# Seven products in place of eight for the second MLP layer of four groups, with a new order of casts, squares and stores

## The chip, the cores and the metric

The kernel runs on one core of a Trainium2 chip. The metric is the device time of one execution in microseconds (us). The kernel before takes 329.64 us in the median. Profiles show the span from the first to the last instruction, some 1.7 us shorter than the time. Engines are named TensorE (PE in the profile, its weight loads PEld), VectorE (DVE), ScalarE (ACT), GpSimd (POOL) and SP, the queue that issues most transfers.

## The reference, cut to what matters

Eight batches of eight heads go through a Nystrom attention with 32 landmarks, and the result goes through an MLP block with layer norm:

```python
x = attn_out.transpose(0, 2, 1, 3).reshape(8, 576, 512)      # 4608 rows of 512
xn = (x - mu) / np.sqrt(var + 1e-06) * g_ln
ch = np.maximum(xn @ w_ch1, 0.0) @ w_ch2                     # 512 -> 2048 -> 512
out = x + ch
```

## The kernel before

The 4608 rows are 36 blocks of 128, in nine groups of four blocks (0 to 8). The attention works on batches in sets: batch 0, batch 1, then set 0 (batch 2), set 1 (batches 3 and 4), set 2 (5 and 6), set 3 (7). The MLP is a generator. Each `fill(n)` takes n of its matmuls and puts them between the steps of the attention, so that TensorE has work while the small attention matmuls wait for other engines. All engines run in the order in which the program was written down.

```python
    # an MLP group: first layer 64 matmuls of 512 columns, second layer 64
    for m in range(MCH):                                     # 16
        psh = psM.tile([P, 512], FP32, name="psh", tag="pm") # three shared banks
        for c in range(KCH):                                 # 4
            MM(psh[:], w1_16[:, c, ts(m, P)], xnT[:, c, :], ...)
        act(hT[:, m, :], psh[:], AF.Relu)
    ...
    for u in range(4):
        for m in range(MCH):
            MM(pso[:], hT[:, m, ts(u, P)], w2_16[:, m, ts(part, n)], ...)
        dve.scalar_tensor_tensor(out=ot[...], in0=pso[:], scalar=rstds[g][:, u:u + 1],
                                 in1=x[...], op0=ALU.mult, op1=ALU.add)
        store(j, ot, ts(part, n))                            # two issues on SP
```

Layer norm is split. Only the mean is taken off before the first layer (`center`, on GpSimd); 1/sqrt(var) is multiplied in after the second layer, because relu lets a positive factor through. For the variance ScalarE makes one `square` for each block. The main loop before (shortened):

```python
    fill(16)
    for c, after, plan in zip(sets, sets[1:] + [None], steps):
        while c.jobs:
            prepare(c, 1, 1)                 # one cast by GpSimd, one transpose or sum by VectorE
            fill(...)
        for (count, jobs), _ in zip(plan, attention2(c.bs, c)):
            fill(count)
            settle()                         # means and centers of finished blocks, by GpSimd
            a_square()                       # one square, by ScalarE
            if after:
                prepare(after, 1, jobs)      # one cast for the next set in every step
```

The softmax here doesn't subtract the row's maximum and nothing guards it: scores larger than these inputs give would overflow.

Of the kernel before, what the change touches and what calls it, by code (L numbers as in the profile page):

```python
# [20 lines left out]
def kernel(  # L21
# [20 lines left out]
    MCH = HID // P  # L42
    U = H // 4
    NJ = 9

    scale_qk = 1.0 / (D ** 0.5)
    sc_A = scale_qk / SEG
# [460 lines left out]
    class Coming:  # L508
# [89 lines left out]

        def spread(self, y):
            part = self.part.pop(y)  # L600
            psl = psM.tile([P, 2, 8, LM], FP32, name="psl", tag="pm")
            for half in range(2):
                MM(psl[:, half, :, :].rearrange("p k c -> p (k c)"),
                   spread16[:, half, :, :, :].rearrange("p e a w -> p (e a w)"),
                   part[:].rearrange("p n w r l x -> p (n w r l x)"))
            lm = asm.tile([P, 8, 2, LM], FP16, name="lm", tag="lm", bufs=3)
            scalar.copy(lm[:].rearrange("p k h c -> p h k c"), psl[:])
            for i, nm in enumerate(("q", "k")):
                for x in range(2):
                    self.lm[nm, 2 * y + x] = lm[:, ds(4 * i + 2 * x, 2), :, :].rearrange(  # L610
                        "p r h (l x) -> p r (h l) x", x=2)
# [118 lines left out]

        yield from rows_of(bs, ea, zcbd)

    ln_ready = {0}
    rowsum, variances, rstds, xn_of = {}, {}, {}, {}
    mlp_at, uncentered = [0], {}
    later, squares, negms = [], [], {}

    def settle():
        while later:
# [1 line left out]

    def block_done(j):
        g, u = divmod(j, 4)
        if g == 0:
            mean_of(j, dve)
            center(j, scalar if u % 2 == 0 else dve)
        elif g == 1:
            mean_of(j, dve)
            later.append(lambda: center(j, scalar))
        else:  # L750
            later.append(lambda: mean_of(j, pool))
            later.append(lambda: center(j, pool) if g <= mlp_at[0] + 1
                         else uncentered.setdefault(g, []).append(j))
        squares.append(lambda: square(j))
        if u == 3:
            if g == 1:
                later.append(lambda: ln_ready.add(1))
            squares.append(lambda: deviations(g))

    def mean_of(j, engine):  # L760
        negms[j] = mstat.tile([P, 1], FP32, name="negm", tag="negm", bufs=16)
# [3 lines left out]
    def center(j, engine):  # L765
        g, u = divmod(j, 4)
        xn_of[j] = xn = mxn.tile([P, DM], FP16, name="xn", tag="xn")
        if engine is scalar:
            act(xn[:], x_blk[j][:], AF.Identity, bias=negms[j][:], scale=1.0)
        elif engine is dve:  # L770
            dve.tensor_scalar(out=xn[:], in0=x_blk[j][:], scalar1=negms[j][:],
                              scalar2=None, op0=ALU.add)
        else:
            pool.tensor_scalar(out=xn[:], in0=x_blk[j][:], scalar1=1.0, scalar2=negms[j][:],
                               op0=ALU.mult, op1=ALU.add)
        if g < 2:
            return
        if u == 0:
            xnTs[g] = mxnT.tile([P, KCH, 512], FP16, name="xnT", tag="xnT")
        keep(nc.sync.dma_start_transpose(out=xnTs[g][:, :, ts(u, P)], in_=xn_of.pop(j)[:]))  # L780

    def square(j):
        g, u = divmod(j, 4)
        if u == 0:
            variances[g] = mstat.tile([P, 4], FP32, name="var", tag="var")
        junk = mxn.tile([P, DM], FP16, name="junk", tag="junk", bufs=1)
        act(junk[:], x_blk[j][:], AF.Square, bias=negms[j][:],
            accum_out=variances[g][:, u:u + 1])

    def deviations(g):  # L790
        lnv = mstat.tile([P, 4], FP32, name="lnv", tag="lnv")
        act(lnv[:], variances.pop(g)[:], AF.Ln, bias=eps_ln[:], scale=1.0 / DM)
        rstds[g] = mstat.tile([P, 4], FP32, name="rstd", tag="rstd")
        act(rstds[g][:], lnv[:], AF.Exp, scale=-0.5)
        ln_ready.add(g)

    def store(j, ot, cols):
        for i in range(2):
            b, c = divmod(2 * j + i, NJ)
            half = ot[ds(64 * i, 64), cols]  # L800
            to = out[b].rearrange("(t j) f -> j t f", j=NJ)[c][:, cols]
            nc.sync.dma_start(out=to, in_=half)

    xnTs = {}

# [15 lines left out]
            yield  # L821



    def mlp():
        for g in range(NGRP):
            mlp_at[0] = g
            hT = mhT.tile([P, MCH, 512], FP16, name="hT", tag="hT")
            if g == 0:
                for m0, u in ([(m, 0) for m in range(0, 12, 2)] + [(m, 2) for m in range(0, 12, 2)]  # L830
                              + [(m, u) for u in (0, 2) for m in (12, 14)]):
                    for t in {(0, 0): (0, 1), (8, 0): (2,), (10, 0): (3,)}.get((m0, u), ()):
                        transpose_block(0, t)
                        yield True
                    psh = psM.tile([P, 2, 256], FP32, name="psh", tag="pm")
                    for m in range(2):
                        for c in range(KCH):
                            MM(psh[:, m, :], w1_16[:, c, ts(m0 + m, P)],
                               xnTs[0][:, c, ds(P * u, 256)],
                               start=(c == 0), stop=(c == KCH - 1), skip=True)  # L840
                            if c == 1 or (c == 3 and m == 0):
                                yield True
                    act(hT[:, m0:m0 + 2, ds(P * u, 256)], psh[:], AF.Relu)
                    yield True
            else:
                while g == 1 and g not in xnTs:
                    if g in ln_ready:
                        for _ in transposes(g):
                            yield True
                    else:  # L850
                        yield False
                while g > 1 and g not in ln_ready:
                    yield False
                xnT = xnTs.pop(g)
                for j in uncentered.pop(g + 1, ()):
                    center(j, pool)
                for m in range(MCH):
                    psh = psM.tile([P, 512], FP32, name="psh", tag="pm")
                    for c in range(KCH):
                        MM(psh[:], w1_16[:, c, ts(m, P)], xnT[:, c, :],  # L860
                           start=(c == 0), stop=(c == KCH - 1))
                        if c < KCH - 1:
                            yield True
                    act(hT[:, m, :], psh[:], AF.Relu)
                    yield True
            tr = None
            for u in range(4):
                j = 4 * g + u
# [28 lines left out]
    def fill(n):  # L897
        for _ in range(n):
            if not next(stream, False):
                return  # L900
# [61 lines left out]
    def prepare(c, casts, jobs):  # L962
        for _ in range(casts):
            if c.casts and (c.parts[c.casts[0]][0] == "v" or len(c.n16) < 8):
                c.next_cast()
                while sum(len(x.stg) for x in sets) < (3):
                    left = [x for x in sets if x.loads]
                    if not left:
                        break
                    left[0].next_load()  # L970
        for _ in range(jobs):
            c.next_job()

    for _ in range(6):
# [1 line left out]

    fills = {"scores of k": 4, "gram": 5, "iteration": 4,
             "product": 5, "zc": 4, "rows": 6}
    def a_square():
        if squares:  # L980
            squares.pop(0)()

    n = 0
    for what in a1:
        fill(fills[what])
        settle()
        if what in ("iteration", "product"):
            a_square()
        if what in ("product", "zc", "rows"):
            n += 1  # L990
            prepare(sets[0], 1, 1 if n > 3 else 0)
    while len(sets[0].jobs) > 1:
        prepare(sets[0], 1, 1)
        fill(6)
    fill(16)

    steps = [[(10, 0), (12, 1)] + 6 * [(6, 1)] + [(8, 1)] + 5 * [(6, 0)]]
    steps += [[(6, 0), (8, 0), (12, 0), (12, 0), (6, 0), (6, 0), (5, 0), (5, 0), (5, 0), (5, 0), (8, 0)] + 3 * [(6, 0)] + 7 * [(7, 1)]]
    steps += [[(12, 0), (14, 1), (16, 1), (16, 1)] + 6 * [(9, 1)] + [(10, 1)] + 10 * [(8, 1)]]
    steps += [[(15, 0), (18, 0)] + 6 * [(12, 0)] + [(12, 0)] + 5 * [(12, 0)]]  # L1000
    for c, after, plan in zip(sets, sets[1:] + [None], steps):
        while c.jobs:
            prepare(c, 1, 1)
            fill(5 if c is sets[1] else 8)
        for (count, jobs), _ in zip(plan, attention2(c.bs, c)):
            fill(count)
            settle()
            a_square()
            if after:
                prepare(after, 1, jobs)  # L1010
    settle()
    while squares:
        a_square()
    for _ in stream:
        pass

# [29 lines left out]
```

## Time and profile before

| | before |
|---|---|
| time, median (lowest to highest) | 329.64 us (328.40 to 330.07) |
| span, mean granted clock | 327.9 us, 0.989 |
| TensorE busy | 312.7 us (95%), 3248 matmuls |
| VectorE, ScalarE, GpSimd busy | 147.7, 153.9, 126.6 us |

TensorE sets the time; the other engines are busy less than half of it. What counts are therefore the matmuls and the places where TensorE stands. The lines that show these are in the prediction.

### The profile page before, as it was taken

To read this page: it belongs to the slowest core of one execution; us is meant where nothing else is said; L and a number is where in the kernel's file an instruction comes from. 1 tells how busy PE (TensorE), PEld (TensorE's weight loads), DVE (VectorE), ACT (ScalarE), POOL (GpSimd) and SP (SyncE) were. 2 spreads that over 40 slices of the span, in tenths; PEclk is the share of its full clock that TensorE was granted. 3 is DMA by queue.
4 is the path that set the end of the run, shared out by engine and by line. 5 is a ranking of instruction groups with operands and counts; after the bars stand their busy time and mean duration, and the time that the engine had idled before them with its cause. 6 is when DMAs were issued, how large, how long until landed. Compare 5 with 4: busy or idle time off the path is not lost.

```text
span 327.9 us, 7900 instructions
## 1 busy us (share of the span) xinstructions
PE 312.7 (95%) x3248; PEld 157.5 (48%) x3248; DVE 147.7 (45%) x392; ACT 153.9 (47%) x301; POOL 126.6 (39%) x194
## 2 busy tenths in 40 slices
PE   8789999899977989999999999999999999999994
PEld 8568654444432534544454445444444444444443
DVE  2667249678782415799366346431232210010012
ACT  2466853587043671567505644583048316305600
POOL 4389879708994796448043011600010300000000
PEclk9999999999995999999999999999999999999999
DMA  7999999559959993933086003520341124032023
GB/s 265 395 386 385 386 389 281 161 109 388 200 133 292 381 246 88 209 113 65 10 213 162 0 18 80 98 35 2 71 98 25 33 67 93 2 79 50 2 56 72
DMA packets 38700, 50.32 MB, mean 153 GB/s; under 512 B 17540, under 2 KB 17800, under 8 KB 38664
## 3 DMA queue, kind: packets, MB, share of 16 engines
q1 hardware_dynamic: 38664, 49.82, 53.6%
q8 instruction: 25, 0.41, 0.6%
q14 instruction: 11, 0.09, 0.1%
HBM read 36.70 MB, written 9.44 MB: 141 GB/s over the span
## 4 chain that ended last, share of the span: by engine, by line
PE 77%; POOL 6%; DMA 5%; DVE 5%; issue 2%; ACT 2%; SPq 1%; POOLq 0%
PE psh L73 35%; PE pso L73 31%; DMA stg<-in_k_dram 2%; PE psy L73 2%; POOL asum L67 2%; PE psn L73 2%; PE pscv L73 2%; DMA xnT<-xn 2%; POOL nat L67 1%; POOL natv L67 1%; DMA stg<-in_q_dram 1%; DVE xblk L67 1%; PE psec L73 1%; DVE part L67 1%; SPq L780 1%
## 5 line engine op out<-in xcount | busy, mean ns | idle before, releaser
L73 PE MATMUL psh<-xnT,w 128*128 128x512 f16 (+1 forms) x640 | 136.3, 360 | 2.0 <-DMA xnT<-xn 2.0
L73 PE MATMUL pso<-w,hT 128*128 128x512 f16 (+1 forms) x592 | 134.5, 375 | 0.0
L67 ACT ACTIVATE hT<-psh 128x512 f16<-128x512 f32 x144 | 85.0, 598 | 89.4 <-PE psh L73 88.8
L73 PEld LDWEIGHTS <-w 128*128 128x128 f16 x640 | 59.2, 98 | 60.5 <-issue 7.3
L73 PEld LDWEIGHTS <-hT 128*128 128x128 f16 x592 | 56.5, 98 | 58.1 <-issue 1.8
L67 DVE SCALAR_TENSOR_TENSOR ot<-pso,rstd,xblk 128x512 f32<-128x512 f32 (+1 forms) x37 | 27.1, 732 | 71.7 <-PE pso L73 68.4
L67 POOL CAST nat<-stg 128x1152 f16<-128x1152 f32 x28 | 31.6, 1145 | 33.4 <-DMA stg<-in_q_dram 30.0
L67 ACT ACTIVATE junk<-xblk,negm 128x512 f16<-128x512 f32 x36 | 25.9, 721 | 30.1 <-POOL negm L67 29.9
L67 POOL TENSOR_SCALAR negm<-rowsum 128x1 f32<-128x1 f32 x28 | 5.3, 190 | 76.8 <-DVE xblk L67 67.6
L67 DVE SCALAR_TENSOR_TENSOR xblk<-psy,rcpd 128x512 f32<-128x512 f32 (+1 forms) x40 | 27.6, 691 | 2.7 <-DVE rcpd L67 0.5
L67 DVE SCALAR_TENSOR_TENSOR st<-st,psn 128x128 f16<-128x128 f16 (+2 forms) x36 | 11.4, 316 | 38.3 <-PE psn L73 38.3
L67 POOL CAST natv<-stg 128x1152 f16<-128x1152 f32 x16 | 18.4, 1161 | 12.1 <-DMA stg<-in_v_dram 12.0
L67 POOL TENSOR_SCALAR xn<-xblk,negm 128x512 f16<-128x512 f32 x28 | 19.2, 692 | 2.0 <-DMA xnT<-xn 0.9
L67 DVE STREAM_TRANSPOSE xT<-nat 128x576 uint32<-128x576 uint32 x24 | 18.4, 768 | 0.0
L67 DVE TENSOR_REDUCE part<-xT 128x32 f16<-128x576 f16 x26 | 18.3, 745 | 0.1
L67 DVE RECIPROCAL rcpd<-psy 128x8 f32<-128x8 f32 (+1 forms) x40 | 8.1, 202 | 20.9 <-PE psy L73 20.8
L73 PE MATMUL psy<-zcbd,ea 128*128 128x260 f16 (+1 forms) x80 | 15.6, 276 | 0.6 <-DVE zcbd L67 0.5
L73 PEld LDWEIGHTS <-st 32*32 32x32 f16 x448 | 5.7, 89 | 16.7 <-issue 11.8
L67 POOL TENSOR_TENSOR asum<-asum 128x256 f32<-128x256 f32 (+1 forms) x22 | 13.0, 591 | 1.7
L67 POOL TENSOR_TENSOR asum<-nat 128x512 f32<-128x512 f16 x11 | 12.7, 1154 | 0.9
L73 PEld LDWEIGHTS <-ea 128*128 128x128 f16 (+1 forms) x80 | 7.2, 100 | 10.9 <-issue 2.6
L67 ACT ACTIVATE ec<-psec 128x576 f16<-128x576 f32 x12 | 8.9, 808 | 7.3 <-PE psec L73 7.3
(101 smaller groups left out, 210.3 us busy)
## 6 DMA issues: line engine op xcount, KB each, us to landing
stg<-in_q_dram SPq DMA_DIRECT2D x16, 576.0 KB, 7.4
stg<-in_k_dram SPq DMA_DIRECT2D x16, 576.0 KB, 7.5
out_dram<-ot SPq DMA_DIRECT2D x70, 128.0 KB, 2.3
wstg<-in_moe_w_ch_dram SPq DMA_DIRECT2D x16, 512.0 KB, 6.9
stg<-in_v_dram SPq DMA_DIRECT2D x10, 576.0 KB, 9.0
stg<-in_v_dram SPq DMA_DIRECT2D x12, 288.0 KB, 9.5
xnT<-xn SPq DMA_TRANSPOSE x28, 2.5
out_dram<-ot SPq DMA_DIRECT2D x4, 64.0 KB, 2.0
```

Source lines behind the costliest of these rows:

```text
L67: return lambda *args, **kw: keep(getattr(self.engine, op)(*args, **kw))
L73: keep(nc.tensor.matmul(o, l, r, start=start, stop=stop, tile_position=(rb, cb), skip_group_check=(skip or cb != 0)))
L780: keep(nc.sync.dma_start_transpose(out=xnTs[g][:, :, ts(u, P)], in_=xn_of.pop(j)[:]))
```

## The change

A product of two matrices, each cut into four blocks, takes eight block products, or seven with sums of blocks (Strassen's scheme). In groups 5 to 8 the second layer becomes seven products of 256 rows x 1024 x 256 columns, that is 7 x 16 = 112 matmuls of 256 columns in place of 64 of 512. For that:

- GpSimd makes four sums of blocks of w2 once. VectorE makes four sums of blocks of h in each group, two of them in own buffers and two over blocks of hT.
- the products are added straight into x, so 1/sqrt(var) must be in h already: groups 5 to 8 are normalized fully before the first layer (`normalize`, on ScalarE, ahead of the center).
- the order changes: 18 fills in place of 16 before set 0; no casts in five steps of set 0 and four of set 1, in which rows come out; squares at least four steps after their block; the second layer, and no longer the first, waits for the variance; the landmarks of the last set use the bank of the iterations (`late`).
- the last four half-block stores are split over the queues of SP and ACT.

The core of the diff:

```diff
+    G_FAST = 5
+            late = self.bs[0] >= 7
+            psl = (ps1 if late else psM).tile([P, 2, 8, LM], FP32, name="psl", ...)
...
+        pa = bank("psp1")
+        yield from product(pa, h11, w11)
+        p1 = mout.tile([P, 2, HN], FP32, name="p1", tag="ot")
+        scalar.copy(p1[:], pa[:])
+        for half, col in ((0, 1), (1, 1), (1, 0)):
+            add(pool, half, col, p1)
+        pb = bank("psp6")
+        yield from product(pb, s2, t2, by_k=True)
+        add(dve, 0, 1, pb)
+        yield from product(pa, h12, w21, False)
+        add(dve, 0, 0, pa)
...
+        (s4, in two halves on VectorE)
+        yield from product(pb, s3, t3, False)
+        add(dve, 1, 1, pb)
+        yield from product(pc, s1, t1)
+        add(dve, 1, 1, pc)
+        yield from product(pb, h22, t4, False)
+        add(dve, 1, 0, pb)
+        c = product(pc, s4, w22, False)
...
-    fill(16)
+    fill(18)
-    steps = [[(10, 0), (12, 1)] + 6 * [(6, 1)] + [(8, 1)] + 5 * [(6, 0)]]
+    steps = [[(10, 1, 0), (12, 1, 1)] + 6 * [(6, 1, 1)] + [(8, 1, 1)] + 5 * [(6, 0, 0)]]
...
-            nc.sync.dma_start(out=to, in_=half)
+            (nc.scalar if both and i else nc.sync).dma_start(out=to, in_=half)
```

## The prediction

> **What bounds the kernel now.** I looked first at the busy time of each engine by stretch, cut where the character of the work changes. Columns: start and end in us, length, then busy us (instructions) of TensorE, weight loads, VectorE, ScalarE, GpSimd, the granted clock, DMA share and GB/s.
>
> ```profile
> 92.00:107.00 15.00, 10.34 (x129) 4.17 (x126) 6.49 (x12) 6.44 (x15) 10.30 (x14) 0.77 0.92 237
> 107.00:126.00 19.00, 17.60 (x384) 8.17 (x370) 5.78 (x18) 11.83 (x22) 16.23 (x21) 1.00 1.03 297
> 126.00:224.00 98.00, 98.00 (x1063) 46.20 (x1063) 58.13 (x152) 52.26 (x109) 31.23 (x54) 1.00 0.38 85
> 224.00:254.70 30.70, 30.70 (x188) 13.58 (x187) 9.42 (x26) 11.80 (x26) 1.45 (x5) 1.00 0.24 52
> 254.70:328.00 73.30, 69.07 (x336) 32.69 (x334) 9.29 (x15) 21.72 (x39) 2.87 (x5) 1.00 0.22 51
> ```
>
> From 126 us to the last matmul TensorE never rests, and no other engine is busy more than 60% (VectorE, 58.13 of 98 us, the most). So a us of matmul taken out after 126 us is a us of time, unless a new wait takes its place. A us of waiting taken out before 126 us is a us too, because everything behind it moves up. The worst stretch is 92 to 107 us: 4.7 us without a matmul, and a clock of 0.77.
>
> The chain that ended last gives the price of the second layer (start, length, what):
>
> ```profile
> 254.66 13.81 PE pso L73 x64
> ...
> 309.91 13.87 PE pso L73 x80
> 323.81 0.48 DVE ot L67
> ```
>
> 64 matmuls of 512 columns take 13.81 us, 215.8 ns each. In the last group one block is cut in two, so 48 are of 512 and 32 of 256 columns: (13.87 - 48 x 0.2158)/32 = 109.7 ns for one of 256 columns with its own weight load. That is the very form the seven products use. After the last matmul come 0.48 us of VectorE, two store issues and the landing, up to 327.9.
>
> Then TensorE in the bad stretch (start, length, instruction, count, in brackets the idle time before it and who ended it):
>
> ```profile
> 92.52 3.40 PE L73 MATMUL pso<-w,hT 128*128 128x512 f16 x15
> 98.58 0.41 PE L73 MATMUL psl<-part,spread 128*128 128x256 f16 x2 [2.66 <-ACT lm L67]
> 98.80 1.47 PE L73 MATMUL pso<-w,hT 128*128 128x512 f16 x3
> 102.27 1.01 PE L73 MATMUL psh<-xnT,w 128*128 128x512 f16 x2 [2.00 <-DMA xnT<-xn]
> ```
>
> Two matmuls in 1.01 us is half speed. Why ScalarE's copy lm is late, and why xnT is late, is seen on ScalarE and GpSimd:
>
> ```profile
> 97.25 0.72 ACT L67 ACTIVATE junk<-xblk,negm 128x512 f16<-128x512 f32 x1 [0.67 <-POOL negm L67]
> 97.88 0.19 ACT L67 ACTIVATION_READ_ACCUMULATOR junk<-xblk,negm 128x1 f32 x1
> 97.97 0.56 ACT L67 CAST lm<-psl 128x512 f16<-128x512 f32 x1
> ```
>
> ```profile
> 75.05 1.15 POOL L67 CAST nat<-stg 128x1152 f16<-128x1152 f32 x1 [11.04 <-DMA stg<-in_q_dram]
> ...
> 93.85 1.16 POOL L67 CAST natv<-stg 128x1152 f16<-128x1152 f32 x1
> 94.97 0.19 POOL L67 TENSOR_SCALAR negm<-rowsum 128x1 f32<-128x1 f32 x1
> 95.26 0.69 POOL L67 TENSOR_SCALAR xn<-xblk,negm 128x512 f16<-128x512 f32 x1
> ```
>
> ScalarE stands on four squares in a row, each waiting for a mean (negm) that GpSimd makes only after another 1.16 us cast of v; the copy lm, for which psl had been ready since 92.7, is behind them. GpSimd itself is late because it had nothing to cast until 75.05. The queue of SP, and VectorE at that time, say why:
>
> ```profile
> 67.65 2.72 SPq L780 DMA_TRANSPOSE xnT<-xn  x1
> 70.43 0.56 SPq L82 DMA_DIRECT2D stg<-in_q_dram  x1
> ```
>
> ```profile
> 65.69 0.71 DVE L67 SCALAR_TENSOR_TENSOR ot<-pso,rstd,xblk 128x512 f32<-128x512 f32 x1
> ```
>
> SP issues in order: the last store of group 0 waits for this ot, a transpose follows, then the load. And ot, whose last matmul ended about 64.0, stands in VectorE's order behind the softmax and two ecT transposes.
>
> **What the Trainium skill says.** "TensorE: Matmul & The Clock Gate", Back-to-back issue gap: N/2.4 + 2.5 ns, so 215.8 ns at 512 columns and 109.2 at 256; the trace agrees (215.8, 109.7). "SBUF — State Buffer", SBUF: two separate sides: a VectorE op with two SBUF inputs and a GpSimd op that reads SBUF exclude each other for a whole instruction. The trace agrees: the eleven small adds part<-sT take 191 to 1205 ns, and the longest (from 95.89, 1.21 us) ends with the 1.16 us cast that GpSimd began at 95.90. "VectorE: DVE Perf Modes", The perf-mode tier table: an elementwise op on two fp16 SBUF tensors runs at two elements a cycle, from PSUM at one; no large one of the first kind is in this trace. "DMA: Bandwidth & Descriptors", Issuing engines are not separate DMA queues: a second issuing engine saves only issue time. Here that is about 0.55 us a store (the last two issues took 1.10 us together).
>
> **The change, part by part.**
> 1. Seven products in groups 5 to 8. Each is 8 x 2 matmuls of 256 columns: 112 x 109.7 = 12.29 us against 13.81. That is 1.52 us for each of three groups and 13.87 - 12.29 = 1.58 for the last: **-6.1 us**, all on the path (these groups run from 224 us on).
> 2. What the products need beside them. For each group VectorE does twelve adds of 128x256 out of PSUM; zcbd<-pszc of that size takes 0.415 us, ot of that size 0.484, so some 5.4 us in place of 4 x 0.746 = 3.0. The four mixes of h have 2048 elements a partition each: with the fixed part of about 0.15 us seen in this trace's ops (0.418 us at 256 elements, one a cycle) I estimate some 6 us at two a cycle, 10 at one. GpSimd does six adds of 0.73 us, ScalarE one copy of about 0.6. VectorE then has 11 to 16 us of work in a group of 26 us: beside TensorE, if the order fits. Walking a group from the end of its first layer, a product is 1.75 us. The tight place is s4: it cannot begin before the third product has ended and been added (6.4 us), and behind it VectorE must add the fourth product out of its bank before the sixth starts there at 8.7. With s4 taking 1.4 us that add ends at 8.6. With s4 at one element a cycle, or blocked by a GpSimd add, it ends up to 1 us late. I put **+0.7 us** for the four groups together.
> 3. The mixes of w2: sixteen GpSimd adds of about 1.15 us in a stretch where it is busy 31 of 98 us. Free. The full normalization adds a square, Ln and Exp of about 1.4 us before each xn, but blocks of groups 5 to 8 are done 10 us or more before their first layer begins. Free.
> 4. Order of rows, casts and squares, around 60 to 107 us. Two more matmuls are put before set 1 of the attention (18 for 16). They fill part of the 0.95 us that TensorE waits at 59.9 (**-0.4**), and they end group 0 before the softmax, so that ot and the store no longer stand behind ecT: SP's transpose and the load of q move up by about 2.5 us, and GpSimd's whole sequence with them. The casts of three v parts move behind the four centers, and the squares come four steps later, so ScalarE is free for lm. By this reckoning the last center that group 2 needs ends at about 91 instead of 95.95, and its transpose lands near 95, no longer beside loads (the old one took 5.1 us, median 2.5). TensorE comes there at about 96.5, so neither wait is left, and without a long rest no half clock. From 95.92, psl, 3 pso, 2 psh, psb/psec, 6 psh, psb/psec need 0.2+0.65+0.43+0.61+1.3+0.61 = 3.8 us and end at 99.7; before they ended at 107.1. That is 7.4 us at most. I take **-6.6**, since the full DMA queues behind it (share 1.03 to 126 us) may hand some back.
> 5. Last stores on two queues: one issue less at the end, **-0.5**.
>
> Sum: 329.6 - 6.1 + 0.7 - 0.4 - 6.6 - 0.5 = 316.7.
>
> **The rivals.** (a) *The waits at 92 to 107 us come back*, as another wait: the DMA share is 1.03 from 107 to 126, and the parts of set 2 are cast only as fast as they land. TensorE arriving 7 us earlier might then wait for them. For it: GpSimd waits for loads at 99, 102 and 109. Against it: the casts end by 125 to 133 and are first needed after 136. If all came back, only the products would count: 323. (b) *VectorE takes the place of the removed matmuls*: if every group lost 1.5 us at a bank that is not yet emptied, the products would give nothing and only the order counts: 322. Against it: 11 to 16 us of work for 26 us. (c) *Weight loads bound the 256-column matmuls*: they take 98 ns each, close to 109. Against it: 32 in a row ran at 109.7, and group 0's first layer runs in that form too. If a product's pace were 120 ns, the four groups would lose 4.6 us of the 6.1: 321.
>
> **Range and chances.** Both parts failing gives about 329, one failing 321 to 323, none failing and no new wait 315. The two gains are independent, so a result above 323.0 (2%) needs nearly one whole part lost. I predict 316.7 us, 312.5 to 321.5, faster by over 2% with 0.93, within 2% 0.06, slower 0.01.
>
> **What would show it.** Right: no wait for lm or xnT around 90 to 105 us and a clock of 1.00 there; the cast of q1 begins near 72.5; each product of sixteen takes 1.75 us, a second layer of 112 matmuls 12.3; TensorE idle below 1 us between 126 us and its end; 3.5 us from the last matmul to the end. Wrong: waits of psp5, psp6 or the next psh for VectorE's adds or mixes in the second layers, an xnT that lands late in groups 5 to 8, a pace above 112 ns, or a clock below 0.95 in some slice after the first.

## The result

The changed kernel takes 319.58 us in the median of four runs (318.81 to 321.8), against 329.64 for the kernel before. The ratio is 0.9712, with a 95% interval of 0.9655 to 0.9768. A ratio here is the mean time of one kernel's runs over that of the other's of the same rounds, so it is not quite the ratio of the medians. Executions over 1.5% slower than the fastest of the same kernel are left out of the means. The kernel is 2.9% faster, and 319.58 lies inside the range (312.5 to 321.5), 2.9 us above the 316.7 predicted.

The profiled run is the fastest of the four: 318.81 us, span 317.1 us, clock 0.997. The same stretches as before the change (start:end, length, busy us and count of TensorE, weight loads, VectorE, ScalarE, GpSimd, clock, DMA share, GB/s):

```profile
92.00:107.00 15.00, 13.06 (x272) 6.11 (x269) 7.16 (x21) 8.68 (x19) 6.83 (x8) 1.00 1.00 253
107.00:126.00 19.00, 17.71 (x291) 7.83 (x282) 6.65 (x19) 8.76 (x17) 17.59 (x23) 1.00 0.96 277
126.00:224.00 98.00, 97.19 (x1065) 47.88 (x1064) 63.03 (x167) 56.59 (x127) 46.06 (x57) 1.00 0.34 82
224.00:254.70 30.70, 30.70 (x241) 20.22 (x239) 18.40 (x53) 15.47 (x37) 10.03 (x13) 1.00 0.24 53
254.70:318.00 63.30, 57.32 (x399) 38.74 (x397) 25.36 (x57) 20.27 (x34) 12.16 (x17) 0.98 0.26 59
```

From 92 to 107 us TensorE is busy 13.06 us where it was 10.34, and the clock is 1.00 where it was 0.77. From 224 us on VectorE has more than twice its old work, and TensorE does not rest. New is a rest of 0.81 us in the third line.

The chain that ended last gives the price of the products (start, length, what):

```profile
273.75 12.23 PE psp L75 x112
285.97 13.81 PE psh L75 x64
299.79 12.25 PE psp L75 x112
312.06 0.42 DVE xblk L69
```

112 matmuls take 12.23 us, 109.2 ns each; the first layer still takes 13.81. After the last matmul (299.79 + 12.25 = 312.04) the kernel needs 5.06 us to its end, where it needed 327.9 - 323.78 = 4.12.

The same piece of work can be found in both chains. The difference between its two times shows where the gain arose and where it was lost:

| work | before, us | after, us | after minus before |
|---|---|---|---|
| group 0's first run of 12 psh (nothing has changed yet) | 28.38 | 27.74 | -0.64 |
| first psec of set 0 | 63.21 | 62.18 | -1.03 |
| first psh behind the second psec of set 1 | 107.17 | 99.42 | -7.75 |
| first psh behind the second pscv of set 1 | 113.33 | 107.46 | -5.87 |
| first psh behind psec of set 3 | 213.04 | 207.90 | -5.14 |
| end of the last matmul | 323.78 | 312.04 | -11.74 |
| end of the span | 327.9 | 317.1 | -10.8 |

So the stretch at 92 to 107 us gave 6.7 us. Of these 1.9 us were lost at once, and 0.7 us by 208 us. The rest of the way to the last matmul gave 6.6 us, and the end took 0.9 us back. The first 0.64 us is the landing of the very first load and not the change. From the second row to the fifth the changed kernel has done two MLP matmuls more at the same place (18 fills for 16), worth 0.43 us, which the kernel before still has ahead of it. So 0.43 of the last 6.6 us belong to the wait before set 0, which these two matmuls fill, and not to the products.

TensorE in the stretch where the gain and the first loss are, and the wait at 180 us (start, length, instruction, count, idle before it and who ended it):

```profile
94.95 0.39 PE L75 MATMUL psl<-part,spread 128*128 128x256 f16 x2
...
95.40 1.03 PE L75 MATMUL psh<-xnT,w 128*128 128x512 f16 x4
...
103.79 0.30 PE L75 MATMUL pscv<-natv,ecT 64*32 64x65 f16 x26 [1.81 <-issue]
...
117.28 0.26 PE L75 MATMUL psn<-st 32*32 32x64 f16 x11 [1.08 <-issue]
...
180.21 0.30 PE L75 MATMUL psn<-st 32*32 32x64 f16 x16 [0.67 <-ACT lm L69]
```

The waits for lm and xnT around 95 us are gone. At 103.79 there is a new wait of 1.81 us whose cause the profile calls "issue": nothing that it shows was missing. The wait of 1.08 us at 117.28 stood in the profile before too, with 1.13 us at 123.20.

The links that the prediction had named, on VectorE, on SP and on GpSimd:

```profile
61.80 0.75 DVE L69 SCALAR_TENSOR_TENSOR ot<-pso,rstd,xblk 128x512 f32<-128x512 f32 x1 [1.35 <-PE pso L75]
```

```profile
66.00 0.58 SPq L84 DMA_DIRECT2D stg<-in_q_dram  x1
```

```profile
70.61 1.15 POOL L69 CAST nat<-stg 128x1152 f16<-128x1152 f32 x1 [6.62 <-DMA stg<-in_q_dram]
...
88.61 0.69 POOL L69 TENSOR_SCALAR xn<-xblk,negm 128x512 f16<-128x512 f32 x1
```

The last ot of group 0 comes 3.9 us earlier (65.69 before), the load of q 4.4 us (70.43), the first late cast 4.4 us (75.05). The last center that group 2 needs ends at 89.30, before at 95.95.

### The profile page after: what moved, and what is told of

Its sections match the earlier page's. It is cut to its first block, busy times and chain, and to the rows that moved or that the text cites. A ratio compares the mean times of both kernels' runs of the same rounds, so it can differ in the third digit from the quotient of the medians.

```text
span 317.1 us, 8390 instructions
## 1 busy us (share of the span) xinstructions
PE 303.6 (96%) x3424; PEld 173.0 (55%) x3424; DVE 179.6 (57%) x487; ACT 161.0 (51%) x329; POOL 161.3 (51%) x218
## 4 chain that ended last, share of the span: by engine, by line
PE 87%; DVE 6%; DMA 2%; issue 2%; ACT 1%; SPq 0%; DVEq 0%
PE psh L75 40%; PE pso L75 19%; PE psp L75 16%; PE psy L75 3%; DMA stg<-in_k_dram 2%; PE psn L75 2%; PE pscv L75 2%; DVE part L69 2%; DVE xblk L69 1%; PE psec L75 1%; DVE ot L69 1%; PE psea L75 1%; DVE xT L69 1%; PE psxt L79 1%; PE pst L79 0%
## 5 line engine op out<-in xcount | busy, mean ns | idle before, releaser
L75 PEld LDWEIGHTS <-hT 128*128 128x128 f16 x640 | 61.1, 98 | 35.0 <-issue 1.4
L75 PE MATMUL pso<-w,hT 128*128 128x512 f16 x320 | 76.5, 379 | 0.0
L69 POOL TENSOR_TENSOR xblk<-p,xblk 128x256 f32<-128x256 f32 x24 | 17.5, 767 | 62.4 <-ACT p L69 62.4
L69 POOL TENSOR_SCALAR xn<-xblk,negm,rstd 128x512 f16<-128x512 f32 x16 | 13.5, 852 | 43.8 <-ACT rstd L69 34.6
L69 DVE TENSOR_TENSOR xblk<-psp,xblk 128x256 f32<-128x256 f32 x48 | 18.1, 418 | 16.1 <-PE psp L75 15.9
L75 PE MATMUL psp<-w,hT 128*128 128x256 f16 x192 | 23.4, 273 | 0.0
L69 DVE TENSOR_TENSOR hmix<-hT 128x256 f16<-128x256 f16 (+2 forms) x16 | 6.8, 424 | 25.6 <-ACT hT L69 25.5
L69 DVE SCALAR_TENSOR_TENSOR ot<-pso,rstd,xblk 128x512 f32<-128x512 f32 x20 | 14.9, 746 | 5.2 <-PE pso L75 5.0
L75 PE MATMUL psp<-w2mix,hT 128*128 128x256 f16 x128 | 15.5, 273 | 0.0
L75 PE MATMUL psp<-w2mix,hmix 128*128 128x256 f16 x128 | 15.3, 273 | 0.0
```

The costliest lines, as they stand in the source:

```text
L69: return lambda *args, **kw: keep(getattr(self.engine, op)(*args, **kw))
L75: keep(nc.tensor.matmul(o, l, r, start=start, stop=stop, tile_position=(rb, cb), skip_group_check=(skip or cb != 0)))
```

## The experiments

Each experiment was compared with the kernel before in its own rounds, whose median was 329.64, 328.47, 328.52 and 330.03 us in the four batches. Every kernel gave correct results.

### The order alone

```diff
-    G_FAST = 5
+    G_FAST = 9
-    mixing = mixes_of_w2()
+    mixing = iter(())
```

> The changed kernel with its threshold of fast groups set past the last group: no products, no mixes, no full normalization, stores at the end as before; the order of rows, casts, squares and the last spread stay. If the two gains are independent, this keeps what the traces show before 224 us: 1.0 us up to set 0, 6.7 us between 92 and 107 us, less the new wait of 1.8 us at the 47th pscv matmul and 0.7 us for lm at 180 us: about 5.2 us, so near 324.4 us, ratio about 0.984. Rival (the order only makes room that the products then use): below 1.5 us of gain.

Measured: 323.95 us, ratio 0.9851 (0.9791 to 0.991); span 323.2 us. From the first layer of group 2 on the trace has the waits of the changed kernel: 1.59 us at the 47th pscv, 0.67 us for lm at 181 us, none for xnT. The theory holds: the order gives about 1.5% by itself (the interval lies below 1, but does not say whether the gain reaches 2%).

### The products alone

```diff
-    fill(18)
+    fill(16)
-    def a_square(least=4):
+    def a_square(least=0):
     # and a cast in every step of sets 0 and 1, as before
```

> The changed kernel with the order of before: 16 units before set 1 of the attention, casts in every step, squares at once. If the gains are independent: 6.3 to 6.6 us from the products less 0.9 us of longer tail, so about 324 us, ratio about 0.983; the waits for lm (2.7 us) and xnT (2.0 us) and the clock below 0.8 around 92 to 107 us come back. Rival (products give nothing without the order, since VectorE then hinders): ratio above 0.992.

Measured: 326.22 us (322.97 to 327.69), ratio 0.9903 (0.9829 to 0.9976), less than expected; the interval holds the expected 0.983 and the 0.992 of the rival alike. The span is 324.0 us. The waits came back as expected, the one for lm shorter, with a clock of 0.77 from 92 to 107 us:

```profile
98.23 0.38 PE L75 MATMUL psl<-part,spread 128*128 128x256 f16 x2 [1.83 <-ACT lm L69]
101.67 1.01 PE L75 MATMUL psh<-xnT,w 128*128 128x512 f16 x2 [2.41 <-DMA xnT<-xn]
```

The last matmul ended near 318.25, 5.5 us earlier than in the kernel before (323.78). The span, however, ended 5.7 us after it, where the kernel before needs 4.1. So the products do give their share on TensorE, and the end takes 1.6 us of it back. The two parts give 1.5% and 1.0%, together 2.9%: within these intervals they add up. Both keep the new bank of the last spread, so both pay its wait of 0.7 us.

### All last stores on two queues

```diff
             for u in (0, 1):
-                store(4 * g + u, x[u], ts(0, HN))
+                store(4 * g + u, x[u], ts(0, HN), True)
...
-                store(4 * g + u, x[u], ts(1, HN))
+                store(4 * g + u, x[u], ts(1, HN), True)
```

> All stores of the last group split over both queues, where the changed kernel splits only the last four. Theory (SP is behind by some 1.2 us with its twelve issues of about 0.58 us when the last block is ready): the last SP issue ends about 1.2 us earlier, the time from the last matmul to the end falls from 5.1 to about 3.9 us, and the time by about 1.1 us. Rival (the ACT queue itself is slow to land, a first use or its own completion): the tail stays at 5 us or grows.

The issues of the last group in the changed kernel, on SP and on the ACT queue (start, length, what, count):

```profile
305.58 8.95 SPq L830 DMA_DIRECT2D out_dram<-xblk  x12
```

```profile
310.84 2.73 ACTq L830 DMA_DIRECT2D out_dram<-xblk  x4
```

In this experiment SP has eight issues, in 7.80 us from 305.93. In the changed kernel VectorE finishes the last block at 312.06 + 0.42 = 312.48, but SP issues until 314.53, because twelve issues of some 0.58 us each have piled up, and the end comes 4.6 us after the last add. Here the last add ends at 312.81, SP issues until 313.73, and the end (316.5) comes 3.7 us after it, as in the kernel before (323.81 + 0.48 to 327.9: 3.6). The 0.9 us is gone. (From the last matmul to the end the changed kernel's store code took 5.1 to 5.7 us in six fast profiles, though 4.2 in the slow one of the shifted program; with all stores split it took 4.1 here and 4.5 in the version below that takes out both small losses.) The time of 319.08 us, ratio 0.9705 (0.9655 to 0.9754), agrees, but the rounds don't resolve it.

### The program moved by 32 rows

```diff
-    warm(36, 160)
+    warm(20, 288)
```

> The warm-up before the first work in 20 matmuls of 288 columns where it was 36 of 160: the same columns, but every later TensorE instruction stands 32 rows (16 matmuls with their loads) earlier in the program. The two longest waits for which the profile names no cause lie at rows 2749 and 3261 of the program, 512 apart, and a short one at 3005 between. Theory (TensorE's instructions come in pieces of 256 rows, 16 KB, and a piece is late when the DMA queues are full): the waits stay at those row numbers, so they move 16 matmuls later in the work: the pscv batch splits 62 and 10 where it split 46 and 26, and the wait in the iterations moves from the sixth psn matmul of the fourth iteration to the first of the fifth. Rival (a dependency of that very instruction that the profile misses): the split stays at 46 and 26. Time within 1% of the changed kernel either way.

```profile
108.22 0.24 PE L75 MATMUL pscv<-natv,ecT 64*32 64x65 f16 x10 [1.87 <-issue]
108.39 4.45 PE L75 MATMUL psh<-xnT,w 128*128 128x512 f16 x12
```

The batch of 72 now splits 62 (at 105.68) and 10, and the later wait (0.72 us, which this profile puts down to psh) stands before the first psn of the fifth iteration. Both are where rows 2749 and 3261 have moved to. So the wait belongs to the place in the program and not to the instruction. The expectation on the time was missed: 317.4 us in one run, but 322.64 to 323.19 in the three others, which are slow, with a clock of 0.978. In the profiled one the warm-up left the clock at 0.87 over the first 40 us, and after the wait the twelve psh took 4.45 us where the changed kernel's take 2.76.

A row here is one TensorE instruction; a matmul is two, its weight load and itself. The rule can be checked in the first two traces. The kernel before has the same wait, split 7 and 9 where the changed kernel has 5 and 11:

```profile
121.83 0.23 PE L73 MATMUL psn<-st 32*32 32x64 f16 x7
123.20 0.26 PE L73 MATMUL psn<-st 32*32 32x64 f16 x9 [1.13 <-issue]
```

Its eighth psn is row 3261 of its program. The changed kernel has two more MLP matmuls, thus four rows, in front, and its sixth psn is row 3261.

### At most two loads on their way

```diff
-                while sum(len(x.stg) for x in sets) < 3:
+                while sum(len(x.stg) for x in sets) < 2:
```

> The changed kernel with at most two loads of q, k, v on their way in place of three. Theory (a piece of 256 TensorE rows, fetched through the same DMA engines, takes about 6.7 us when the queues are full, and TensorE runs through it sooner): with shorter queues the pieces come sooner, so the waits at rows 2749, 3005 and 3261 shrink from 1.8, 0.2 and 1.1 us to less than half in sum; the casts may come later, so the time may still not fall. Rival (the pieces come at a pace of their own, whatever the queues hold): the waits stay within 0.3 us of what they were.

Measured: no wait is left at rows 2749, 3005 and 3261, so fewer loads in the queues do remove it, and the theory holds. TensorE did not come later than in the changed kernel: it went from row 2493 to 2749, 3005 and 3261 in 5.06, 6.35 and 5.48 us, where the changed kernel with its waits needed 6.94, 6.74 and 6.75. The DMA share stayed at 0.95 and 1.00 in these stretches, so the share alone does not tell whether there is a wait. One of 0.49 us called "issue" appeared at 97.20, but at row 2395 of the program, not at a block's end. But the casts for set 2 are later, and the centers of group 3 behind them:

```profile
139.26 3.17 PE L75 MATMUL psh<-xnT,w 128*128 128x512 f16 x7 [5.54 <-DMA xnT<-xn]
```

The time is 325.79 us, ratio 0.9918 (0.9864 to 0.9972): the cure costs more than the illness.

### The kernel before with 18 in place of 16

```diff
-    fill(16)
+    fill(18)
```

> The kernel before with one number changed: 18 units of the MLP before set 1 of the attention in place of 16. Theory (the root of the stretch of 92 to 107 us is that the load of q stands on SP behind the last store of group 0, whose ot stands on VectorE behind the softmax): the load is issued about 4 us earlier (66 where it was 70.4), GpSimd's casts and centers move up by as much, lm is copied before it is missed and xnT lands before it is needed, even with the casts and squares in the old order: nearly the whole 6 us of the order come from this number, about 323.5 us, ratio 0.98 to 0.985, no lm or xnT wait above 1 us. Rival (moving the casts and delaying the squares is what removes the waits): lm still waits 2 us or more and the time stays above 326 us.

```profile
96.38 0.39 PE L73 MATMUL psl<-part,spread 128*128 128x256 f16 x2 [0.99 <-DVE part L67]
99.22 1.75 PE L73 MATMUL psh<-xnT,w 128*128 128x512 f16 x4 [2.23 <-DMA xnT<-xn]
```

Measured: 325.17 us, ratio 0.9856 (0.9794 to 0.9918), near what was expected for the time, but not in the way expected. The load of q is issued at 66.98 and the wait for lm is gone; the wait for xnT stays at 2.23 us, with a clock of 0.89 from 92 to 107 us. The third center ends at 93.14, where the changed kernel's ends at 89.30. Neither the theory (no wait above 1 us) nor the rival (lm still waits) is right.

### The changed kernel with 16 in place of 18

```diff
-    fill(18)
+    fill(16)
```

> The changed kernel with 16 units in place of 18, so the casts and squares keep their new order and only the load of q goes back behind the softmax. Theory: SP issues it near 70, the first late cast begins near 75, the four centers end near 94 and the transpose lands near 97, about when TensorE comes: a wait for xnT of 0 to 1.5 us, no wait for lm since no square stands before it, and the 0.9 us wait for part is back: 1 to 2.5 us slower than the changed kernel, about 321.5. So either part alone would remove most of the waits. Rival (the number is everything): both waits back, 5 us slower, 325.

Measured: 319.46 us, ratio 0.9712 (0.967 to 0.9754), the ratio of the changed kernel itself. The load of q comes at 69.26 and the third center ends at 92.40, yet no wait for lm or xnT is left at 92 to 107 us:

```profile
92.00:107.00 15.00, 14.32 (x296) 6.71 (x295) 7.92 (x21) 8.68 (x18) 7.25 (x9) 1.00 0.94 221
```

Besides the wait at 180 us, four short waits stand in their place: 0.89 and 0.43 us for part, 0.59 us at row 3261, and 0.77 us for the xnT of group 3. So the number 18, in which the prediction saw the root, is not needed once casts and squares are in their new order. The changed gate on the variance plays no part in this: TensorE's MLP matmuls stand in the same order among the psl and psy of the attention as in the kernel before, up to the second layer of group 5.

### 16 units, with casts or squares in the old order

```diff
-    fill(18)
+    fill(16)
     # f16_casts_old: and a cast in every step of sets 0 and 1
     # f16_squares_old: and
-    def a_square(least=4):
+    def a_square(least=0):
```

> The changed kernel with 16 units and the casts in the old places (one in every step, so the casts of v stand between the centers); only the delay of the squares and what belongs to the products stay. Theory (the casts are what makes xnT late, the squares are what makes lm late): the last center that group 2 needs ends near 95.9 again, TensorE waits 2 us or more for xnT, but lm is copied at once, no wait for it. About 322 to 323 us. Rival (the delay of the squares alone cures both, since nothing else has changed on ScalarE): no xnT wait above 1 us, time as the changed kernel.

Measured: the profile fell into a disturbed execution of 610.67 us and can't be read for waits: runs of eight 256-column matmuls took 1.95 us in it, and 1.05 in the profile before, although the clock column says 1.00. The runs classed fast took 324.97 and 325.14 us; the median of all four is 328.05, the ratio of the fast runs 0.9891 (0.9817 to 0.9964). Against 319.46 us with the casts moved this is a loss of more than 5 us, larger than expected. That the casts matter is shown; that it is by way of xnT is only argued here.

> The changed kernel with 16 units and the squares at once, the casts in their new places. Theory: with the casts behind the centers the means are ready by about 93, so the squares keep ScalarE only briefly: no lm wait above 0.7 us, no xnT wait above 1.5 us, time within 0.4% of the changed kernel, so the squares' delay is worth nothing once the casts have moved. Rival (the delay is needed by itself): an lm wait of 2 us or more.

Measured: 319.72 us, ratio 0.9717 (0.9666 to 0.9768), no wait for lm before 170 us and none for xnT below group 3 (0.94 us there). The delay of the squares is worth nothing once the casts have moved. This run has at most 0.07 us of wait at rows 2749, 3005 and 3261, with three loads on their way, and is no faster: waits of 0.96 and 0.84 us for part and the one for xnT stand in their place.

### The spread of the last set back in the shared banks

```diff
-            late = self.bs[0] >= 7
+            late = False
```

> The changed kernel with the spread of the last set in the three shared banks, as before, and not in the single bank of the iterations. Theory: the 0.67 us wait of a psn for lm at 180 us goes, since the psn no longer shares its bank with psl, and nothing comes in its place: PE's last matmul 0.5 to 0.7 us earlier, 0.2% in time, which the rounds may not resolve. Rival (the move was needed, because a bank of the shared three is then missed by the products): a new wait of psh or psp of 0.5 us or more after 180 us.

Measured: 318.91 us, ratio 0.9713 (0.9656 to 0.977), span 317.0. The wait at 180 us is gone and no other came in its place after 126 us. The single bank of the iterations was what psn had waited for. The last matmul ended at 311.26, 0.8 us earlier, but the end took 5.7 us in place of 5.06, so the span is only 0.1 us shorter. That the move was a small loss is shown on TensorE, and not in the time.

### Both small losses taken out

This kernel has the edits of the two-queue stores and of the last spread together.

> The changed kernel with all last stores on two queues and the spread of the last set back in the shared banks, the two small losses that the first runs showed together. Theory: 0.9 us less tail and 0.7 us less wait at 180 us: a span near 315.5, time about 0.5% below the changed kernel, ratio to before about 0.966. Rival (they hide behind each other or the waits for instructions grow by as much): ratio 0.970 or above.

Measured: 317.74 us in six runs (317.26 to 318.44), ratio 0.967 (0.9627 to 0.9713), span 316.1 us, no wait for lm at 180 us, last matmul at 311.64. Its median is 1.8 us below that of the changed kernel. It has the lowest median here, but its interval shares more than half of its width with that of the changed kernel, which ran in other rounds; in the same rounds f16_squares_old took 319.72 us (318.18 to 319.82). The 4.0 us from the last add (311.66 + 0.42) to the end are not as short as the 3.7 us of the experiment on the stores alone.

### Group 4 too

```diff
-    G_FAST = 5
+    G_FAST = 4
-                        if m == 0:
+                        if m == 12:
                             while not h_mix:
-                for _ in range(1):
+                for _ in range(3):
                     next(mixing, None)
```

> As best5, and group 4 too by the seven products: three mixes of w2 in a step in place of one, so that they are ready by its second layer, and the wait for the buffers of the h mixes moved to the thirteenth tile of the first layer. Theory: one more group saves 1.58 us of matmul, nothing new waits: a span near 314, ratio about 0.961. Rival (GpSimd cannot make sixteen mixes of about 1.15 us before some 185 us, or blocks of x stay longer and the rows of set 2 wait for a buffer): a wait of 1.5 us or more for w2mix or xblk between 160 and 215 us and no gain over best5.

Measured: five of six runs took 324.36 to 325.03 us, ratio 0.9882 (0.9838 to 0.9925), about 7 us slower than the version with four groups. The sixth, the profiled one, was disturbed (545.73 us, matmuls at half their pace), so the wait that costs the 7 us was not seen. The clock of the five, 0.989 to 0.993, is below the 0.995 to 1.000 of the version with four groups, which fits a longer rest of TensorE but does not show where. This stays open.

## Why the prediction was right

The direction, the size and both sources were right; the sum was 12.9 us, and 10.8 came in the profile, 10.06 in the medians. By its terms:

| term | predicted, us | in the two profiles, us |
|---|---|---|
| products, with new waits of VectorE | -6.1 + 0.7 | -6.4, and +0.2 not traced |
| wait at 59.9 us | -0.4 | -0.8 |
| 92 to 107 us | -6.6 | -6.7, then +1.9 |
| lm at 180 us | none | +0.7 |
| stores on two queues | -0.5 | +0.9 |
| first load | none | -0.6 |

**The products.** The price from the cut block, 109.7 ns, was right: 109.2 ns. The groups gave 3 x 1.58 + (13.87 - 12.25) = 6.36 us. The stretch behind 208 us gave 6.60; with the 0.43 us of the two matmuls that were already done, 0.19 us less came than the sum of both, and this was not traced. The new wait did not come, but the place that the prediction named tight is tight. VectorE and TensorE in the last group:

```profile
305.13 0.76 DVE L69 TENSOR_TENSOR xblk<-psp,xblk 128x256 f32<-128x256 f32 x2 [0.95 <-PE psp L75]
305.81 1.84 DVE L69 TENSOR_TENSOR hT<-hT,hmix 128x1024 f16<-128x1024 f16 x2
307.57 1.41 DVE L69 TENSOR_TENSOR xblk<-psp,xblk 128x256 f32<-128x256 f32 x4
```

```profile
308.37 1.91 PE L75 MATMUL psp<-w2mix,hT 128*128 128x256 f16 x16
```

The two halves of s4 take 1.84 us here, 1.24 and 0.68. Over the four groups they take 924 ns in the mean, where the same shape takes 684 to 692 ns in the other mixes: the five halves that run into one of GpSimd's adds took 829 to 1243 ns, the three others 677 to 679. The first two of the four adds that follow end near 307.57 + 2 x 0.38 = 308.3, and the product that needs their bank begins at 308.37. The prediction had put that add at 8.6 and the product at 8.7 us from the start of the layer; it was 8.5 and 8.6.

**The wait at 59.9 us.** In the profile of the changed kernel it is gone altogether. In six other profiles with 18 fills and the new order 0.47 to 0.54 us of it stay, as was predicted, so half of the 0.8 us is the luck of one execution.

**The stretch of 92 to 107 us.** The gain was right in size, and every link that was named moved as said. The weight of the links was wrong. The prediction made the load of q, and with it the number 18, the root. The experiments show that, of the three moves, the casts alone remove both waits (16 units with the squares at once: 319.72 us), and that 18 without them leaves a wait of 2.23 us for xnT. The prediction's sentence "they end group 0 before the softmax" describes a true chain, but one that is not needed. The delay of the squares was also counted as a cause, and it has no worth of its own.

**What was handed back.** The step that failed is "I take -6.6, since the full DMA queues behind it [...] may hand some back". Handing back was foreseen, through casts that wait for loads; its size was set at 0.8 us and it was 1.9, and the way was another. TensorE's own instructions came late. Its program has 6848 rows (3424 matmuls, each with its load), and the profile counts 27 transfers of kind "instruction" with 0.44 MB on one queue, so some 254 rows each. The waits stand at rows 2749, 3005 and 3261, 256 apart, in the kernel before, the changed one and seven of the experiments (not all three in each), and they moved with the rows when the program was shifted. They disappear with fewer loads. The packed trace of the changed kernel has each of these transfers with its time. Those before the three rows land at 102.41, 108.98 and 115.79, and TensorE goes on 1.38, 1.56 and 1.48 us later. Each takes 0.9 to 1.4 us, no more than the others in the trace. It is their start that is late: 3.9 to 4.7 us after TensorE has entered the block before, where it was 2.3 to 3.1 us with fewer loads, and 0.9 us for the block at row 4029, at a low DMA share. What holds the start up inside the queues is not shown.

In the changed kernel the waits at these rows end at 103.79, 110.53 and 117.28 us, 6.74 and 6.75 us apart; the last two in the kernel before end at 116.46 and 123.20, 6.74 apart. TensorE with its small attention matmuls is quicker than that. In the kernel before the stretch was slowed by its other waits, so the block at row 2749 came in time (it landed 2.15 us before TensorE was there); when those were removed, this one appeared.

**The end.** The sign was wrong. The step was "one issue less at the end, -0.5". It looked at the last store alone. But the new second layer stores half blocks, sixteen issues in the last group in place of ten, and twelve of them stand on SP, which ends its issues 2.05 us after the last add; one issue takes some 0.58. Splitting all of them gave 0.9 us back. The sign "3.5 us from the last matmul to the end" was missed: it was 5.06.

**The wait at 180 us** was not foreseen: the diff's move of the last spread was passed over. It cost 0.7 us on TensorE, and no wait came when it was taken back; the time did not resolve it.

The rivals: (a), a return of the waits in another form, came true for 1.9 of the 6.7 us, not for all. (b) and (c), VectorE or the weight loads as the new bound, did not come: no wait for either in the second layers.

## What to carry to other kernels

Take the price of a new matmul form from a place in the trace where the same form already runs in a row; it was right to half a percent. When several moves act on one wait, undo each alone before naming the root: here the one that looked like the first link could be left out. When a wait of some us is removed from a stretch with full DMA queues and many small instructions, count the instructions of that stretch, because their own transfer can be the next limit, and count all issues at the end of a kernel and not only the last.

## What the Trainium skill lacked or had wrong

- "Runtime: NRT & Kernel Launch", Instruction fetch mechanics, says that instructions are refilled in blocks of 256 and that the cost of a block boundary is mostly hidden. The blocks agree (rows 2749, 3005, 3261). Hidden they were not when their transfers started late: waits of 1.81 and 1.08 us in the changed kernel and 1.87 in the shifted one. In the changed kernel the transfers behind them took 0.9 to 1.4 us, but began 3.9 to 4.7 us after TensorE had entered the block before.
- "DMA: Bandwidth & Descriptors", Issuing engines are not separate DMA queues, says that a second issuing engine saves only issue time, which is usually small. It is so for one store (about 0.58 us); for sixteen half-block stores at the end it was worth 0.9 us of the tail.
- "SBUF — State Buffer" and "VectorE: DVE Perf Modes" agree on what the prediction took from them: a mix of 1024 fp16 elements took 0.69 us, with a fixed part of 0.15 two elements a cycle, and the halves of s4 that ran into GpSimd's adds took 0.83 to 1.24.
- "TensorE: Matmul & The Clock Gate", Back-to-back issue gap, gives the formula that the prediction took for an isolated matmul, and some 131 ns at 512 columns for a sustained stream. Here 64 in a row, each with its own weight load, took 13.81 us, 215.8 ns each: the stream ran at the formula's pace and not at 131.
- The same page, Seeing it yourself, warns that clock events in a trace can be unreliable. No page has executions like the two disturbed ones here (610.67 and 545.73 us, both with matmuls at half their pace, the first with a clock column of 1.00); what caused them was not found.
